# Middle and backward of an attention block in a fixed order: side work in small parts, quarter products, prefetch into dead tiles

## The chip, the cores and the metric

The kernel runs on one core of one Trainium2 chip; the chip's other cores are idle. The metric is the device time of one execution in microseconds (us). A number of executions is made, and the median is given with its range. The span of a profile is one execution, from its first to its last instruction.

Engines: PE is the matmul engine (PEld its weight loads), DVE the vector engine, ACT the scalar engine, POOL the engine that starts the output stores here, SP the engine that starts most loads. A profile lists each engine's instructions in order of time, with the idle time before each and what ended it.

## The reference, cut to what matters

One token goes through a modulated block with attention over a cache of 8192 positions, 32 heads of 192 numbers, all in bf16. The kernel returns the output and nine gradients.

```python
mod = silu(c) @ w_mod                       # w_mod: 640 x 3840, six vectors of 640
sa, ca, ga, sb, cb, gb = split(mod, 6)
h  = layernorm(x) * (1 + ca) + sa
q  = h @ wq                                 # wq: 640 x 6144
p  = softmax(q . K / sqrt(192))             # K, V: 32 x 8192 x 192
x  = x + ga * ((p @ V) @ wo)                # wo: 6144 x 640
h  = layernorm(x) * (1 + cb) + sb
x  = x + gb * mlp(h)                        # mlp holds w3: 640 x 1536, w4: 1536 x 640
# (that is the forward; then the gradients)
out, vjp = jax.vjp(f, x, K, V, wq, wo, w3, w4, c, w_mod)
return out, *vjp(grad_out)
```

Most bytes are K and V (100.7 MB each), read in the forward. The backward reads V again and writes dK and dV, of the same sizes. In all 347.74 MB are read from HBM and 226.43 MB written.

## The kernel before: the parts that matter

A cache of one head is handled in two halves, 128 partitions x 32 positions x 192 (1.5 MB). There are 64 half heads. The kernel has three stages: the forward over all heads; the "middle", which does the MLP and its backward on single vectors; and the backward over the half heads.

The names in the extracts: `V_` is DVE, `A_` ACT, `T_` PE. `P` = 128, `D` = 640, `DH` = 192, `JH` = 32, `HQ` = 32, `NT` = 16 pairs of heads, `ND` = 5, `NF` = 12, `CW` = 768 columns of a weight tile, `PW` = 384.

The middle loads w3 and w4 and reduces d(g) on DVE, twelve times:

```python
with tc.tile_pool(name="mid", bufs=1) as mid, tc.tile_pool(name="mst", bufs=2) as mst:
    w3_sb = mid.tile([P, ND, F], BF16, name="w3_sb")
    nc.sync.dma_start(out=w3_sb, in_=B_w3.rearrange("(i p) n -> p i n", p=P))
    ...                                            # w4_sb likewise; w3 transposed on PE
    bcast_cols(dbo, ND, dbo_bc, A_.copy)
    for a in range(NF):
        junk = mst.tile([P, D], BF16, name="junk")
        V_.tensor_tensor_reduce(out=junk, in0=w4_sb[:, a, :], in1=dbo_bc, scale=1.0, scalar=0.0,
                                op0=ALU.mult, op1=ALU.add, accum_out=d_g[:, a : a + 1])
    ...                                            # layer norms, MLP, their backward, dw3, dw4
```

One half head of the backward. The scheduler of the language decides the order of instructions on each engine, the program order gives only the dependencies and a preference:

```python
for h in range(HQ):
    for t in range(2):
        v = load_v(h, t)                           # 1.5 MB
        dP = tcol(JH, "dP")
        dot_sum(dot_tree(dot_mul(v, doh), psR, DH), dP)   # DVE product, PE adds 12 slices, DVE reduces
        V_.scalar_tensor_tensor(out=dS4, ...)      # (dP - cpr) * E
        dV = ob.tile([P, JH, DH], BF16, name="dV", tag="o")
        outer_v(dV, load_er(h, t), doh)            # 32 matmuls on PE, 8 copies on ACT
        nc.gpsimd.dma_start(out=dV_hd[h][:, js, :], in_=dV)
        dK = ob.tile([P, JH, DH], BF16, name="dK", tag="o")
        times(dK, qh, dS4, 0, JH)                  # DVE
        nc.gpsimd.dma_start(out=dK_hd[h][:, js, :], in_=dK)
        for f in side.get(2 * h + t, ()):          # side work of this half head
            f()
```

The side work is: `do` (dO of the next two heads: wo tile, 15 transposes, matmuls), `dq` (a tile of wq: transposes, matmuls, an outer product, dwq), `dwo`, and `wm` (a tile of w_mod, treated as one of wq). The tile of wq or w_mod has only one buffer:

```python
def load_w(view3, lo, hi):
    w = wst.tile([P, ND, CW], BF16, name="w_st", tag="w", bufs=1)      # 0.98 MB
    nc.sync.dma_start(out=w[:, :, 0 : hi - lo], in_=view3[:, :, lo:hi])
    return w

def half_chunk(view, n, b, v3, rows, dst, acc, lay):
    lo = n * CW
    if b == 0:
        cur["w"] = load_w(view, lo, lo + CW)
        cur["stg"] = bst.tile([P, ND, CW], BF16, name="stg")
    ...
    outer_chunk(cur["w"][:, :, sl], v3, rows, cur["stg"][:, :, sl], acc, lay)   # transposes w on PE, ...
    if b == 1:
        nc.gpsimd.dma_start(out=dst[:, :, lo : lo + CW], in_=cur["stg"])
```

Of the kernel before, what the change touches and what calls it, by code (L numbers as in the profile page):

```python
# [20 lines left out]
def kernel(  # L21
# [47 lines left out]
    assert DH == 192 and HQ % 4 == 0 and J % 16 == 0 and JH * TS <= 512  # L69
    assert D % P == 0 and F % P == 0 and NMOD % CW == 0  # L70
# [7 lines left out]
    pp = ctx.enter_context(tc.tile_pool(name="pp", bufs=1))  # L78
    PS = bass.MemoryType.PSUM
    psB = ctx.enter_context(tc.tile_pool(name="psB", bufs=1, space=PS))  # L80
    psS = ctx.enter_context(tc.tile_pool(name="psS", bufs=1, space=PS))
    dram = ctx.enter_context(tc.tile_pool(name="dram", bufs=1, space=bass.MemoryType.DRAM))
# [32 lines left out]
    def mean_cols(src, groups, name):  # L115
        n = groups * ND
        ps = psS.tile([P, 16], FP32, name="mean_ps", tag="s")
        T_.matmul(ps[:, 0:n], lhsT=onesD, rhs=src, start=True, stop=True)
        m = tcol(groups, name)
        V_.reduce_sum(out=m, in_=ps[:, 0:n].rearrange("p (a b) -> p a b", b=ND), axis=AX.X)  # L120
        return m

    def layernorm(x, name):
        m = mean_cols(x, 1, name + "_m")
# [4 lines left out]
        var = mean_cols(sq, 1, name + "_v")  # L129
# [125 lines left out]
    dbo = col(ND, "dbo")  # L255

# [25 lines left out]
    NKB = 5  # L282
    NVA = (7 * JQ) // 16
    MO = 256
    with tc.tile_pool(name="kp", bufs=1) as kp, tc.tile_pool(name="vs", bufs=3) as vsp, tc.tile_pool(name="ft", bufs=2) as ft, \
            tc.tile_pool(name="psM", bufs=2, space=PS) as psM, tc.tile_pool(name="psO", bufs=2, space=PS) as psO, \
            tc.tile_pool(name="psR", bufs=2, space=PS) as psR:
        KB = [None] * NKB
        for k in range(NKB):
            b = (2 * (HQ - 1) + 2 + k) % NKB  # L290
            KB[b] = kp.tile([P, JH, DH], BF16, name=f"KB{b}")

# [94 lines left out]
        ORDER = {mybir.EngineType.PE, mybir.EngineType.DVE, mybir.EngineType.Activation, mybir.EngineType.SP}  # L387
# [7 lines left out]
        with tc.manual_schedule(engines=ORDER):  # L395
            for i in range(HQ + 2):
                x = X.get(i)
# [34 lines left out]
                if x is not None:  # L432
                    x["v"].append(load_v(i, 1))
                if z is not None:
                    mt = m_out(i - 2, z["mp"], z["op"], os_)
# [33 lines left out]
                if i % 4 == 0 and mb < NMB:  # L469
                    nb = min(CW // P, NMB - mb)  # L470
                    wch = load_w(wm_v, mb * P, (mb + nb) * P)
                if y is not None:
                    m_quarter(2, y["k"][1], vs, y["mp"], y["op"])
                if x is not None:
                    dot_sum(x["d0"], x["S"][:, 0:JH])
                if y is not None:
                    y["vs"] = scale_v(3, y["v"][1], E4, Ef)
                if nx is not None:
                    nx["v"].append(load_v(i + 1, 0))
            while mb < NMB:  # L480
                nb = min(CW // P, NMB - mb)
                mod_blocks(mb, nb, load_w(wm_v, mb * P, (mb + nb) * P))
                mb += nb
    V_.tensor_tensor(out=dbo, in0=dy_c, in1=gb, op=ALU.mult)
# [8 lines left out]
    ckS = col(NQ, "ckS")  # L493
    psV = ctx.enter_context(tc.tile_pool(name="psV", bufs=2, space=PS))
    psR = ctx.enter_context(tc.tile_pool(name="psR2", bufs=1, space=PS))
    psT = ctx.enter_context(tc.tile_pool(name="psT", bufs=1, space=PS))
    with tc.tile_pool(name="mid", bufs=1) as mid, tc.tile_pool(name="mst", bufs=2) as mst:
        w3_sb = mid.tile([P, ND, F], BF16, name="w3_sb")
        nc.sync.dma_start(out=w3_sb, in_=B_w3.rearrange("(i p) n -> p i n", p=P))
        w4_sb = mid.tile([P, NF, D], BF16, name="w4_sb")  # L500
        nc.sync.dma_start(out=w4_sb, in_=B_w4.rearrange("(a p) r -> p a r", p=P))
        w3T = mid.tile([P, NF, D], BF16, name="w3T")
        for g in range(0, NF, 3):
            tp = psV.tile([P, 2048], BF16, name="w3T_ps", tag="v")
            for a in range(3):
                for k in range(ND):
                    T_.transpose(out=tp[:, a * D + k * P : a * D + (k + 1) * P], in_=w3_sb[:, k, (g + a) * P : (g + a + 1) * P], identity=ident_bf)
            A_.copy(out=w3T[:, g : g + 3, :], in_=tp[:, 0 : 3 * D].rearrange("p (a r) -> p a r", a=3))
        dbo_bc = mid.tile([P, D], BF16, name="dbo_bc")
        bcast_cols(dbo, ND, dbo_bc, A_.copy)  # L510
        d_g = mid.tile([P, NF], FP32, name="d_g")
        for a in range(NF):
            junk = mst.tile([P, D], BF16, name="junk")
            V_.tensor_tensor_reduce(out=junk, in0=w4_sb[:, a, :], in1=dbo_bc, scale=1.0, scalar=0.0, op0=ALU.mult, op1=ALU.add, accum_out=d_g[:, a : a + 1])

        ao = mid.tile([P, ND], FP32, name="ao")
        V_.reduce_sum(out=ao, in_=AO, axis=AX.X)
        x1 = mid.tile([P, ND], FP32, name="x1")
        V_.tensor_tensor(out=x1, in0=ga, in1=ao, op=ALU.mult)
        V_.tensor_tensor(out=x1, in0=x1, in1=x_c, op=ALU.add)  # L520
        n1, r1 = layernorm(x1, "ln1")
        h_b = mid.tile([P, ND], FP32, name="h_b")
        V_.scalar_tensor_tensor(out=h_b, in0=cb, scalar=1.0, in1=n1, op0=ALU.add, op1=ALU.mult)
        V_.tensor_tensor(out=h_b, in0=h_b, in1=sb, op=ALU.add)
        n2, r2 = layernorm(h_b, "ln2")
        n2_bf = tcol(ND, "n2_bf", BF16)
        V_.tensor_copy(out=n2_bf, in_=n2)
        ups = psS.tile([P, NF], FP32, name="u_ps", tag="s")
        for a in range(NF):
            for k in range(ND):  # L530
                T_.matmul(ups[:, a : a + 1], lhsT=w3_sb[:, k, a * P : (a + 1) * P], rhs=n2_bf[:, k : k + 1], start=(k == 0), stop=(k == ND - 1))

        def fcol(name, dtype=FP32):
            return mid.tile([P, NF], dtype, name=name)

        u, u2, w_, s_, g_, du = (fcol(n) for n in ("u", "u2", "w_", "s_", "g_", "du"))
        V_.tensor_copy(out=u, in_=ups)
        V_.tensor_tensor(out=u2, in0=u, in1=u, op=ALU.mult)
        V_.tensor_scalar(out=w_, in0=u2, scalar1=GELU_K1, scalar2=1.0, op0=ALU.mult, op1=ALU.add)
        V_.tensor_tensor(out=w_, in0=w_, in1=u, op=ALU.mult)  # L540
        A_.activation(out=w_, in_=w_, func=ACT.Exp, scale=-2.0 * GELU_K0)
        V_.tensor_scalar(out=w_, in0=w_, scalar1=1.0, scalar2=None, op0=ALU.add)
        V_.reciprocal(out=s_, in_=w_)
        V_.tensor_tensor(out=g_, in0=s_, in1=u, op=ALU.mult)
        g_bf = fcol("g_bf", BF16)
        A_.copy(out=g_bf, in_=g_)

        t_, v_ = fcol("t_"), fcol("v_")
        V_.tensor_scalar(out=t_, in0=s_, scalar1=-2.0 * GELU_K0, scalar2=2.0 * GELU_K0, op0=ALU.mult, op1=ALU.add)
        V_.tensor_tensor(out=t_, in0=t_, in1=g_, op=ALU.mult)  # L550
        V_.tensor_scalar(out=v_, in0=u2, scalar1=3.0 * GELU_K1, scalar2=1.0, op0=ALU.mult, op1=ALU.add)
# [285 lines left out]
```

## Time and profile before

The time is 1517.53 us (median of three runs, 1516.53 to 1517.59). The profiled execution has a span of 1520.6 us.

| stage | DMA share | GB/s | PE clock granted |
|---|---|---|---|
| forward, 80 to 540 us | 1.00 | 404 | 0.99 |
| middle, 560 to 660 us | 0.58 | 208 | 0.68 |
| backward, 700 to 1440 us | 0.98 | 393 | 0.57 |

The table is taken from the view of stage windows of the kernel before. Its columns are: the window, its length, the busy time (and instructions) of PE, PEld, DVE, ACT and POOL, then the granted clock of PE, the share of the 16 DMA engines, and GB/s.

```profile
80.00:540.00 460.00, 424.49 (x6207) 326.99 (x6206) 433.88 (x403) 337.55 (x1071) 7.72 (x14) 0.99 1.00 404
560.00:660.00 100.00, 62.62 (x776) 43.92 (x777) 49.27 (x141) 44.21 (x95) 9.94 (x16) 0.68 0.58 208
700.00:1440.00 740.00, 578.92 (x3509) 200.24 (x3509) 478.36 (x575) 404.50 (x550) 75.87 (x132) 0.57 0.98 393
```

The forward keeps the DMA engines full (1.00). The middle leaves them partly idle (0.58), so time cut from it should be time won. The backward has the DMA engines at 0.98, with PE busy 78% at a granted clock of 0.57.

The chain of waits of the kernel before, from 540 to 760 us (start, length, what held up the end at that time), shows what the middle waits for:

```profile
576.97 11.57 DMA w_sb<-in_B_w_dram
...
595.13 0.73 DVE junk L514
...
596.61 0.74 DVE junk L514
```

After the forward's last matmuls the load of w3 and w4 stands alone on the chain for 11.57 us, and the twelve d(g) reductions follow at 0.74 us each, about 9 us.

The groups of waits of the kernel before, from 655 to 1505 us (engine, line, what it waited for: us in total, times, longest us):

```profile
DVE dP L279 <- PE dot_ps L275: 242.0, 60, 16.9
...
PE wT_ps L628 <- DMA w_st<-in_w_mod_dram: 26.8, 4, 16.2
...
PE wT_ps L628 <- DMA w_st<-in_A_wq_dram: 13.5, 3, 8.4
```

DVE waits 242 us for the sums on PE. In four places PE waits for a tile of w_mod and in three for one of wq, 40.3 us in all. The timeline of the kernel before shows the longest of them (start, length, engine, line, operation, in brackets the idle time before it and what ended it):

```profile
741.57 0.38 SPq L182 DMA_DIRECT2D w_st<-in_w_mod_dram  x1
...
766.23 1.04 PE L628 MATMUL wT_ps<-ident_bf,w_st 128*128 128x128 bf16 x8 [16.20 <-DMA w_st<-in_w_mod_dram]
```

A load of 0.98 MB that is issued at 741.57 feeds its first matmul at 766.23, 24.7 us later.

A half head of the backward ends with its store of dK, so the starts of the 64 dK stores, read from the timeline of POOL, give 63 periods. Before, the first store is at 655.2 us and the last at 1504.8: a mean period of 13.49 us.

### The profile page before, as it was taken

Reading aid. Unit: us, or ns where it says so; the run is one execution under the profiler, and the core shown is the slowest. Engines: PE = TensorE matmul, PEld = TensorE weight load, DVE = VectorE, ACT = ScalarE, POOL = GpSimd, SP = SyncE. Lnnn points to the kernel's source line nnn. Section 1 sums busy time; section 2 is a strip of 40 time slices with the busy share of each in tenths; the row PEclk is TensorE's granted clock in tenths of the full one; section 3 lists DMA queues with packets and bytes.
Section 4 is the critical chain, followed back from the end, with each engine's and each line's share of the span. In section 5 each row is a group of like instructions: output and inputs, shape, how many; then the busy total and the mean of one; then the engine's idle time right before and its main releaser. Section 6 shows DMA issues by size and latency. Waiting matters only on the chain.

```text
span 1520.6 us, 28209 instructions
## 1 busy us (share of the span) xinstructions
PE 1209.5 (80%) x11811; PEld 645.4 (42%) x11811; DVE 1105.0 (73%) x1273; ACT 895.9 (59%) x1948; POOL 108.0 (7%) x193
## 2 busy tenths in 40 slices
PE   3999999998999995477668788776887788777773
PEld 1776777776776775233223223222222222222210
DVE  5999999999999975476747576675656666667663
ACT  1776777767776774255445556554555555545554
POOL 0000000000000000101001010110100010110011
PEclk7999999999999997566655555675555555556555
DMA  9999999999999985498989999999999999999978
GB/s 379 401 402 419 414 414 406 398 398 402 391 414 399 390 331 208 161 366 338 427 351 368 404 395 410 418 423 387 381 385 378 404 364 379 375 402 404 401 309 357
DMA packets 76478, 575.99 MB, mean 379 GB/s; under 512 B 7327, under 2 KB 25071, under 8 KB 35391
## 3 DMA queue, kind: packets, MB, share of 16 engines
q1 hardware_dynamic: 51530, 347.23, 57.6%
q0 software_dynamic: 24288, 226.44, 36.4%
q8 instruction: 92, 1.51, 0.4%
q10 hardware_dynamic: 532, 0.53, 0.1%
q14 instruction: 36, 0.29, 0.0%
HBM read 347.74 MB, written 226.43 MB: 378 GB/s over the span
## 4 chain that ended last, share of the span: by engine, by line
issue 33%; PE 23%; DVE 22%; ACT 10%; DMA 7%; POOL 4%; SPq 0%; POOLq 0%; ACTq 0%; DVEq 0%
DVE prod L264 11%; PE dot_ps L275 10%; ACT vs L319 5%; DVE prod L269 3%; DVE vs L312 3%; PE mp L326 3%; DMA w_st<-in_w_mod_dram 2%; PE dv_ps L737 2%; DVE S_h L279 2%; ACT dV L738 2%; PE mp L330 2%; PE wT_ps L628 2%; POOL out_dram L799 1%; POOL out_dram L796 1%; DMA w_st<-in_A_wq_dram 1%
## 5 line engine op out<-in xcount | busy, mean ns | idle before, releaser
L275 PE MATMUL dot_ps<-prod,ident_bf 128*128 128x512 bf16 x1152 | 464.9, 532 | 86.6 <-DVE prod L269 46.5
L738 ACT CAST dV<-dv_ps 128x768 bf16<-128x768 f32 x512 | 387.9, 809 | 211.0 <-PE dv_ps L737 198.5
L319 ACT ACTIVATE vs<-v_sb,Ef 128x192 bf16<-128x192 bf16 x896 | 323.4, 443 | 0.0
L737 PE MATMUL dv_ps<-do_bc,er_b 1*128 1x192 bf16 x2048 | 221.3, 327 | 57.4 <-ACT dV L738 56.7
L275 PEld LDWEIGHTS <-ident_bf 128*128 128x128 bf16 x1152 | 115.7, 114 | 265.5 <-issue 232.1
L279 DVE TENSOR_REDUCE dP<-dot_ps 128x32 f32<-128x512 f32 x64 | 44.2, 690 | 245.4 <-PE dot_ps L275 245.3
L264 DVE TENSOR_TENSOR prod<-KB,qs_bc 128x6144 bf16<-128x6144 bf16 x64 | 214.4, 3350 | 9.9 <-DMA KB<-in_A_k_cache_dram 5.5
L742 DVE TENSOR_TENSOR dK<-qs_bc,dS 128x6144 bf16<-128x6144 bf16 x64 | 214.1, 3346 | 8.2 <-DMA out_dram<-dK 8.1
L264 DVE TENSOR_TENSOR prod<-v_sb,do_bc 128x6144 bf16<-128x6144 bf16 x64 | 214.2, 3347 | 3.5 <-ACT do_bc L679 3.5
L326 PE MATMUL mp<-vs,KB 128*128 128x193 bf16 x2048 | 198.8, 250 | 0.5 <-ACT vs L319 0.5
L737 PEld LDWEIGHTS <-er_b 1*128 1x128 bf16 x2048 | 64.9, 102 | 295.7 <-issue 293.0
L326 PEld LDWEIGHTS <-KB 128*128 128x128 bf16 x2048 | 178.6, 99 | 20.6 <-issue 6.0
L312 DVE TENSOR_TENSOR vs<-v_sb,E 128x1728 bf16<-128x1728 bf16 x128 | 131.7, 1050 | 0.7 <-ACT E L300 0.6
L269 DVE TENSOR_TENSOR prod<-prod 128x3072 bf16<-128x3072 bf16 x64 | 112.1, 1751 | 0.6
L330 PE MATMUL mp<-vs,KB 128*64 128x193 bf16 x2048 | 109.8, 250 | 0.0
L628 PE MATMUL wT_ps<-ident_bf,w_st 128*128 128x128 bf16 (+1 forms) x470 | 51.8, 289 | 70.9 <-DMA w_st<-in_w_mod_dram 26.8
L330 PEld LDWEIGHTS <-KB 128*64 128x64 bf16 x2048 | 82.0, 109 | 20.8 <-issue 20.8
L796 POOL DMA_DIRECT2D out_dram<-dV x64 | 35.4, 554 | 669.9 <-ACT dV L738 669.9
L629 ACT COPY wqT<-wT_ps 128x1024 bf16<-128x1024 bf16 (+1 forms) x52 | 50.4, 970 | 49.0 <-PE wT_ps L628 39.6
L628 PEld LDWEIGHTS <-w_st 128*128 128x128 bf16 (+1 forms) x470 | 37.7, 132 | 91.3 <-issue 47.4
L300 ACT ACTIVATE E<-S_h,negm 128x256 bf16<-128x256 f32 x32 | 16.3, 508 | 91.1 <-DVE negm L421 91.1
L334 PE MATMUL op<-vs,ones_bf 128*32 128x193 bf16 x2048 | 66.2, 250 | 0.0
(207 smaller groups left out, 863.1 us busy)
## 6 DMA issues: line engine op xcount, KB each, us to landing
v_sb<-in_A_v_cache_dram SPq DMA_DIRECT2D x128, 1536.0 KB
KB<-in_A_k_cache_dram SPq DMA_DIRECT2D x64, 1536.0 KB
out_dram<-dV POOLq DMA_DIRECT2D x64, 1536.0 KB, 9.2
out_dram<-dK POOLq DMA_DIRECT2D x64, 1536.0 KB, 13.3
w_st<-in_A_wq_dram SPq DMA_DIRECT2D x16, 960.0 KB
wo_st<-in_A_wo_dram SPq DMA_DIRECT2D x32, 480.0 KB
out_dram<-stg POOLq DMA_DIRECT2D x13, 960.0 KB, 14.5
w_st<-in_w_mod_dram SPq DMA_DIRECT2D x8, 960.0 KB
```

The lines of the kernel that those rows point to most:

```text
L264: V_.tensor_tensor(out=prod, in0=src, in1=vec[:, None, :].to_broadcast([P, JH, DH]), op=ALU.mult)
L269: V_.tensor_tensor(out=prod[:, :, 0:w], in0=prod[:, :, 0:w], in1=prod[:, :, w : 2 * w], op=ALU.add)
L275: T_.matmul(ps, lhsT=ident_bf, rhs=prod[:, :, k : k + TS], start=(k == 0), stop=(k == w - TS))
L279: V_.reduce_sum(out=dst, in_=ps, axis=AX.X)
L312: V_.tensor_tensor(out=vs[:, 0:n, 0:DH].rearrange("p j (a b) -> p j a b", b=4), in0=v[:, v0 : v0 + n, :].rearrange("p j (a b) -> p j a b", ...
L319: A_.activation(out=vs[:, k, 0:DH], in_=v[:, v0 + k, :], func=ACT.Copy, scale=Ef[:, j0 + k : j0 + k + 1])
L326: T_.matmul(mp[:, 0:MW], lhsT=kb[:, j0 + k, 0:P], rhs=vs[:, k, 0:MW], start=(q == 0 and k == 0), stop=(z and k == JQ - 1), skip_group_chec ...
L330: T_.matmul(mp[p0 : p0 + 64, MO : MO + MW], lhsT=kb[:, j0 + k, P:DH], rhs=vs[:, k, 0:MW], start=False, stop=(z and k >= JQ - 2), skip_grou ...
L628: T_.transpose(out=tp[lo:hi, (x - x0) * P : (x - x0 + 1) * P], in_=src, identity=ident_bf)
L737: T_.matmul(ps[:, b, k * DH : (k + 1) * DH], lhsT=er[p0 : p0 + 1, 2 * m + k, :], rhs=doh[p0 : p0 + 1, :], start=True, stop=True)
L738: A_.copy(out=dV4[:, 2 * q : 2 * q + 2, m * PW : (m + 1) * PW], in_=ps[:, :, 0:PW])
L742: V_.tensor_tensor(out=out3[:, n0_:n1_, :].rearrange("p j (a b) -> p j a b", b=4), in0=vec.rearrange("p (a b) -> p a b", b=4)[:, None, :, ...
```

## The change: intent and diff

The change tries four things. (1) In the middle, d(g) moves into the last head of the forward, and w3, w4, the first wo tiles and three V tiles are loaded early, into K tiles that have died. (2) The backward's product is made in two quarters, so that the next half head's sum on PE may run beside this half head's dK on DVE. (3) The side work is cut into small parts, and these are dealt evenly over four slots in each half head. (4) The order of the instructions on PE, DVE, ACT and SP is fixed to the order of the program (`manual_schedule`) for the middle and the backward, too.

The core of the diff (`...` marks cuts):

```diff
+    KB = [kp.tile([P, JH, DH], BF16, name=f"KB{b}") for b in range(NKB)]
+    KX, KY, KC, KD, KE = (KB[(2 * HQ + k) % NKB] for k in (-4, -5, -3, -2, -1))
+    OB = (KE, KC, KY, KX)                        # the output tiles of the backward
+    do_bc = flat(KD)[:, 0:QD]
     ...
+            def dg_part(n):
+                for a in dgs[:n]:
+                    V_.tensor_tensor_reduce(out=junk, in0=w4r(a), in1=dbo_bc, ..., accum_out=d_g[:, a : a + 1])
+                del dgs[:n]
             for i in range(HQ + 2):
+                if i == HQ:
+                    ...                          # loads of w4, w3, a V tile, wo; d_bo broadcast
     ...
+                if i == HQ:
+                    dg_part(6)
                 if y is not None:
                     m_quarter(2, y["k"][1], vs, y["mp"], y["op"])
     ...
                 if y is not None:
                     y["vs"] = scale_v(3, y["v"][1], E4, Ef)
+                if i == HQ:
+                    dg_part(6)
     ...
+    ctx.enter_context(tc.manual_schedule(engines=ORDER))
     ...
+    def next_w():
+        if wseq:
+            view, n = wseq.pop(0)
+            cur["next"] = load_w(view, n * CW, (n + 1) * CW)
     ...
+    def g_chunk(b, v3, rows, dst, n, acc, lay):  # five parts, one per yield
+        if b == 0:
+            cur["w"] = cur.pop("next")
+        ...
+        yield
+        transposed(0, cols, ND, wT)              # part 2: first read of the weight tile on PE
+        ...
+        yield
+        transposed(8, cols, ND, wT)              # part 3: last read
+        if b == 1:
+            next_w()                             # the next tile's load, into the same buffer
+        ...
+        yield
+        ...                                      # parts 4 and 5
     ...
+    for t in range(NT):
+        if t > 0:
+            jobs.append((1, g_dwo(t)))
+        if t + 3 < NT:
+            jobs.append((3, g_do(t + 3)))
+        jobs.append((5, g_dq(t)))
+        if t % 2 == 0:
+            wseq.append((wq_v, t // 2))
+        if t % 4 == 3 and late:
+            wseq.append((wm_v, late[0]))
+            jobs.append((10, g_wm(late.pop(0))))
     ...
+    SLOTS = 4 * (NS - 5)
+    def slot():                                  # deals the side parts out evenly
+        prog[0] += 1
+        while prog[1] * SLOTS < NP * prog[0] and prog[1] < NP:
+            next(side)
+            prog[1] += 1
     ...
+    for s in range(NS):
+        ...                                      # reduction of dP, dS
+        slot()
+        dv_groups(dV, er, doh, (0, 1, 2, 3))
+        if nxt:
+            mul_q(s + 1, 0)                      # quarter product of the next half head, on DVE
+            tree_q(ps, 0)                        # its sum, on PE
+        slot()
+        dk_part(dK, qh, dS4, 0, JQ)
+        dv_groups(dV, er, doh, (4, 5))
+        slot()
+        dv_groups(dV, er, doh, (6, 7))
+        nc.gpsimd.dma_start(out=dV_hd[h][:, ...], in_=dV)
+        if nxt:
+            mul_q(s + 1, 1)
+            tree_q(ps, 1)
+        if s + 4 < NS:
+            v_l[s + 4] = load_v((s + 4) // 2, s % 2)
+        if s + 2 < NS:
+            er_l[s + 2] = load_er(s + 2)
+        dk_part(dK, qh, dS4, JQ, JH)
+        nc.gpsimd.dma_start(out=dK_hd[h][:, ...], in_=dK)
+        slot()
```

## The prediction

> **What bounds the kernel now.** The slices and stage windows show three stages.
> - Forward, 80-540 us: DMA share 1.00, 404 GB/s, TensorE clock 0.99. DMA-bound; the change does not touch it.
> - Middle, 560-660 us: DMA share 0.58, 208 GB/s. The chain of waits holds the load of w3/w4 (11.6 us after the last forward matmul), twelve d(g) reductions of 0.74 us on DVE (595.1-604.1), then dw3/dw4/dO preparation. The first dV goes out at 650.7 us, the first dK at 655.2.
> - Backward, 700-1440 us: DMA share 0.98, 393 GB/s; clock 0.57 (many slices 0.50[...]). Stores of dK run from 655.2 to 1504.8, 63 periods of 13.5 us. With no side work (1434-1483) a period is still 12.3 us at DMA share about 0.83: a serial chain of product (3.35), PE tree interleaved with dV matmuls (about 7.8), reduction 0.69, dS 0.34. DVE waits 234 us there for the tree. Side work adds stalls to that chain, and one 18.7 us hole (674-692) in which a w_mod load and side matmuls block PE.
>
> Best 10-80 us windows of the backward give 420-427 GB/s, so 393 is not the ceiling ([...]the trace comes to 427).
>
> **What the change does, costed.**
> 1. Middle: d(g) goes to the last head, where DVE is a third busy: -9 us. w3/w4, three V tiles and wo are prefetched into dead K tiles: about -3 us. dw3, du broadcast, dwo, x2 leave the path; dw4 goes to ACT (12 x about 0.5 us, off the chain). Against it: dn waits behind transposes, h2 matmuls sit before the layer-norm backward on PE (about +2). I put the first dV store at 622 us and the first dK at 626: -28 us.
> 2. Backward: quarter products (two of 1.7 us) let the next half's tree run beside this half's dK. Engine work per half stays: PE about 11 us cold (tree 5.1, dV 3.4, side 2.5), ACT 8.5, DVE 9.3. In the new order I estimate a PE-to-ACT-to-PE chain of about 12.2 us with side parts.
> 3. DMA then binds. About 342 MB remain for 64 halves, 5.34 MB each: 12.6 us at 424 GB/s, 13.2 at 405. I take 13.0: -31 us over 63 periods.
> 4. End: the last dK's landing, 15.8 us before, about 14: no large change. er loads join the SP queue: no cost expected while V prefetch runs ahead.
>
> Sum: 626 + 63 x 13.0 + 14 = 1459, with a little less if the first halves run in the DMA's slack: **1455 us** (-4%). Range 1428-1488.
>
> Chances: faster by over 2%: 0.88; within 2%: 0.10; slower: 0.02.
>
> **What the profile would show.** First dV store near 622 (wrong if after 635). d(g) off the middle's chain. Backward windows at DMA share 1.0 and 405-425 GB/s, clock still 0.5-0.6, period 12.8-13.2 us; DVE's wait for the tree falls from 234 us below 120; waits for output-tile stores appear on ACT and DVE; no hole like 674-692. Forward unchanged within 3 us.
>
> **What would make it wrong.** A saturated rate that is 390 rather than 415 with stores at 60% of the traffic (then about 1485). The fixed order making PE wait for an ACT copy of a side part, with the clock at 0.50 throughout: an engine-bound period over 13.3. SP's ordered queue holding a V load behind a weight or er load. On the other side: a warmer clock and 425 GB/s, about 1430.

"Cold" and "a warmer clock" mean no more here than a lower and a higher granted clock in the traces: 0.50 from 1434 to 1483 us, where the view gives a DMA share of 0.80 rather than 0.83, and 0.57 from 700 to 1440 us. The 5.1 us of the tree and the 3.4 us of dV fit PE's pace in the first of these stretches: from 1447.04 us on, four dV matmuls pass in 0.43 us and then five of the tree in 2.25 us, so 32 and 12 of them take 3.4 and 5.4 us by my estimate. The 0.5 us for a dw4 instruction on ACT was an estimate; the trace of the changed kernel has them at 0.82 us.

## The result, and the profile after

The changed kernel takes 1497.40 us (median of four runs, 1496.22 to 1498.64), and the kernel before, in the same rounds, 1517.56 (1516.53 to 1520.06). The ratio is 0.9865, with a 95% interval of 0.9848 to 0.9882. Ratios in this text are the mean time of one kernel's fast runs over that of the other's of the same rounds, so they are not quite the ratio of the medians that are quoted. The gain is 1.35%, where 4% was predicted, and 1497 lies outside the range.

The stage windows of the changed kernel, with two slices of 20 us beneath:

```profile
80.00:540.00 460.00, 424.34 (x6182) 326.55 (x6181) 436.49 (x405) 338.92 (x1076) 7.69 (x14) 0.99 1.00 405
560.00:660.00 100.00, 72.15 (x847) 53.19 (x845) 55.27 (x123) 58.69 (x123) 7.79 (x13) 0.70 0.68 253
700.00:1440.00 740.00, 518.41 (x4244) 310.58 (x4242) 499.75 (x736) 399.63 (x559) 80.60 (x138) 0.59 0.97 393
...
1000.00:1020.00 20.00, 7.46 (x55) 4.36 (x54) 6.99 (x9) 6.91 (x10) 1.09 (x2) 0.50 0.94 392
1020.00:1040.00 20.00, 15.91 (x129) 9.82 (x128) 12.42 (x16) 11.85 (x17) 1.05 (x2) 0.59 0.73 267
```

The forward is unchanged, the middle is denser, and the backward moves the same 393 GB/s as before. In the slice from 1000 to 1020 us PE, DVE and ACT are busy 35 to 37% of the time, and in the next one the DMA engines go down to 0.73 of their time and 267 GB/s.

The stores of dK split the span into the start (up to the first store), the 63 periods, and the drain (from the last store to the end):

| kernel | first dK store | 63 periods, sum | mean | median | over 20 us | drain | span |
|---|---|---|---|---|---|---|---|
| before | 655.2 | 849.6 | 13.49 | 12.9 | six, 20.2 to 28.5 | 15.8 | 1520.6 |
| predicted | 626 | 819 | 13.0 | | | 14 | 1459 |
| after | 630.1 | 854.8 | 13.57 | 12.9 | 23.1, 23.6, 27.8 | 10.2 | 1495.2 |

From before to after, the start is 25.0 us shorter, the backward 5.2 us longer, the drain 5.6 us shorter: 25.4 us of span. Against the prediction the start is 4 us longer, the backward 36 us longer, and the drain 4 us shorter. The three long periods exceed the median by 10.2 + 10.7 + 14.9 = 35.8 us. So the miss has the size of three holes.

The groups of waits of the changed kernel, from 655 to 1505 us, name what they are:

```profile
DVE vrow L774 <- PE bc_t L772: 98.2, 22, 15.0
DVE dP L290 <- PE dot_ps L695: 86.5, 53, 5.1
...
DVE KB L711 <- DMA out_dram<-KB: 37.3, 11, 6.0
...
PE wT_ps L582 <- DMA w_st<-in_w_mod_dram: 33.5, 3, 14.9
...
PE wT_ps L582 <- DMA w_st<-in_A_wq_dram: 2.2, 1, 2.2
```

DVE's wait for the sums on PE fell from 242.0 to 86.5 us, as the quarter products intended. But in three places PE waits for a w_mod tile, up to 14.9 us. These three waits add to 33.5 us, close to the 35.8 us by which the long periods exceed the median. All waits of PE for weight tiles were 40.3 us before and are 35.7 now: the change hardly touched them. A wait of DVE for the small transpose (bc_t) that PE issues right after the tile's transposes grew as well, from 17.9 us before to 98.2. The timeline of the changed kernel around the first of the three:

```profile
992.69 0.38 SPq L188 DMA_DIRECT2D w_st<-in_w_mod_dram  x1
...
1003.08 0.56 POOL L938 DMA_DIRECT2D out_dram<-KB  x1 [4.91 <-ACT KB L707]
...
1013.75 1.03 PE L582 MATMUL wT_ps<-ident_bf,w_st 128*128 128x128 bf16 x8 [9.18 <-DMA w_st<-in_w_mod_dram]
...
1014.88 1.01 ACT L583 COPY wT<-wT_ps 128x1024 bf16<-128x1024 bf16 x1 [12.09 <-PE wT_ps L582]
1015.03 0.28 DVE L774 CAST vrow<-bc_t 3x128 bf16<-3x128 f32 x1 [12.97 <-PE bc_t L772]
...
1026.47 0.53 POOL L938 DMA_DIRECT2D out_dram<-KB  x1 [22.05 <-ACT KB L707]
```

One late tile stops four engines in a row. PE has the transposes next in its stream and waits 9.18 us. ACT has the copy of their result next and waits 12.09; DVE has the copy of bc_t next and waits 12.97; POOL has no output to store for 22.05 us. The period is 23.1 us, 10.2 over the median, which is about PE's wait. Work that did not depend on the tile stood behind these instructions: the sums for DVE's next dP were done on PE by 1004.57 us (1001.83 + 2.74 in the same timeline), yet its reduction began at 1015.24, behind the copy of bc_t; PE's next dV matmuls began at 1016.79, behind the transposes, and ACT's next dV copies at 1018.05, behind the copies of the transposes. The three tiles take 21.1, 21.1 and 24.9 us from issue to first use.

The end of the forward, in the timelines of first the kernel before and then the changed one:

```profile
563.61 0.51 ACT L300 ACTIVATE E<-S_h,negm 128x256 bf16<-128x256 f32 x1 [0.49 <-DVE negm L421]
...
581.01 0.32 DVE L517 TENSOR_REDUCE ao<-AO 128x5 f32<-128x160 f32 x1 [0.90 <-ACT AO L456]
```

```profile
565.32 0.51 ACT L314 ACTIVATE E<-S_h,negm 128x256 bf16<-128x256 f32 x1 [0.90 <-DVE negm L459]
...
578.40 1.05 DVE L326 TENSOR_TENSOR vs<-v_sb,E 128x1728 bf16<-128x1728 bf16 x1
...
579.51 1.99 PE L340 MATMUL mp<-vs,KB 128*128 128x193 bf16 x16 [3.14 <-DVE vs L326]
...
587.39 0.32 DVE L605 TENSOR_REDUCE ao<-AO 128x5 f32<-128x160 f32 x1 [0.90 <-ACT AO L496]
```

From the last softmax to the reduction of the attention's output it was 17.4 us and is 22.1. The chain of waits of the changed kernel (start, length, what) says why:

```profile
575.05 0.83 DVE w4b L414
...
577.65 0.82 DVE w4b L414
578.49 0.98 DVE vs L326
```

These are d(g) reductions, now in the last head. They stand on the chain ahead of the last scaling of V, for which PE then waits 3.14 us.

### The profile page after: what moved, and what is told of

The parts are those of the page before. It is cut to its first block, busy times and chain, and to the rows that moved or that the text cites. A ratio compares the mean times of both kernels' runs of the same rounds, so it can differ in the third digit from the quotient of the medians.

```text
span 1495.2 us, 30163 instructions
## 1 busy us (share of the span) xinstructions
PE 1143.8 (77%) x12579; PEld 773.2 (52%) x12579; DVE 1121.6 (75%) x1391; ACT 891.5 (60%) x1966; POOL 106.7 (7%) x190
## 4 chain that ended last, share of the span: by engine, by line
issue 52%; DVE 19%; PE 12%; ACT 9%; POOL 6%; DMA 1%; POOLq 0%; SPq 0%; DVEq 0%; ACTq 0%
DVE prod L275 9%; ACT vs L333 6%; DVE vs L326 4%; DVE prod L280 3%; PE mp L340 3%; PE dot_ps L286 2%; POOL out_dram L938 2%; POOL out_dram L948 2%; DVE S_h L290 2%; PE mp L344 2%; PE q_ps L248 1%; PE op L348 1%; DMA KB<-in_A_k_cache_dram 1%; PE po L378 1%; POOL out_dram L796 1%
## 5 line engine op out<-in xcount | busy, mean ns | idle before, releaser
L707 ACT CAST KB<-dv_ps 128x768 bf16<-128x768 f32 x512 | 377.3, 813 | 167.5 <-PE dv_ps L706 152.9
L695 PE MATMUL dot_ps<-pq,ident_bf 128*128 128x256 bf16 x1536 | 327.9, 398 | 57.9 <-DVE pq L686 57.9
L706 PE MATMUL dv_ps<-KB,er_b 1*128 1x192 bf16 x2048 | 179.2, 319 | 145.2 <-ACT KB L707 137.0
L695 PEld LDWEIGHTS <-ident_bf 128*128 128x128 bf16 x1536 | 203.4, 136 | 161.3 <-issue 90.0
L711 DVE TENSOR_TENSOR KB<-qs_bc,dS 128x3072 bf16<-128x3072 bf16 x128 | 223.8, 1749 | 37.4 <-DMA out_dram<-KB 37.3
L686 DVE TENSOR_TENSOR pq<-v_sb,KB 128x3072 bf16<-128x3072 bf16 x128 | 223.7, 1748 | 0.0
L275 DVE TENSOR_TENSOR prod<-KB,qs_bc 128x6144 bf16<-128x6144 bf16 x64 | 214.5, 3352 | 10.2 <-DMA KB<-in_A_k_cache_dram 5.5
L583 ACT COPY wT<-wT_ps 128x1024 bf16<-128x1024 bf16 x84 | 81.0, 964 | 200.6 <-PE wT_ps L582 197.2
L286 PE MATMUL dot_ps<-prod,ident_bf 128*128 128x512 bf16 x384 | 97.3, 391 | 46.6 <-DVE prod L280 46.6
L344 PEld LDWEIGHTS <-KB 128*64 128x64 bf16 x2048 | 82.8, 110 | 21.1 <-issue 21.1
L582 PE MATMUL wT_ps<-ident_bf,w_st 128*128 128x128 bf16 (+1 forms) x470 | 51.7, 293 | 44.0 <-DMA w_st<-in_w_mod_dram 33.5
L286 PEld LDWEIGHTS <-ident_bf 128*128 128x128 bf16 x384 | 36.0, 99 | 89.4 <-issue 60.5
L774 DVE CAST vrow<-bc_t 3x128 bf16<-3x128 f32 x26 | 7.2, 278 | 98.2 <-PE bc_t L772 98.2
L938 POOL DMA_DIRECT2D out_dram<-KB x64 | 36.4, 569 | 589.5 <-ACT KB L707 589.3
## 6 DMA issues: line engine op xcount, KB each, us to landing
out_dram<-KB POOLq DMA_DIRECT2D x128, 1536.0 KB, 13.1
```

The costliest lines, as they stand in the source:

```text
L275: V_.tensor_tensor(out=prod, in0=src, in1=vec[:, None, :].to_broadcast([P, JH, DH]), op=ALU.mult)
L286: T_.matmul(ps, lhsT=ident_bf, rhs=prod[:, :, k : k + TS], start=(k == 0), stop=(k == w - TS))
L344: T_.matmul(mp[p0 : p0 + 64, MO : MO + MW], lhsT=kb[:, j0 + k, P:DH], rhs=vs[:, k, 0:MW], start=False, stop=(z and k >= JQ - 2), skip_grou ...
L686: V_.tensor_tensor(out=pq[:, q], in0=v_l[s][:, q * JQ : (q + 1) * JQ, :], in1=do_bc[:, None, (s // 2) * DH : (s // 2 + 1) * DH].to_broadca ...
L695: T_.matmul(ps[:, q * JQ : (q + 1) * JQ, :], lhsT=ident_bf, rhs=pq[:, q, :, k : k + TS], start=(k == 0), stop=(k == DH - TS), skip_group_c ...
L706: T_.matmul(ps[:, b, k * DH : (k + 1) * DH], lhsT=er[p0 : p0 + 1, 2 * m + k, :], rhs=doh[p0 : p0 + 1, :], start=True, stop=True)
```

## The experiments

Twelve kernels were run. Unless it is said otherwise, each differs from the changed kernel in one thing and gives the reference's result. "Over 20 us" counts the long periods between dK stores in the profiled execution.

| run | median us (range) | ratio to before [95%] | mean period | median period | over 20 us |
|---|---|---|---|---|---|
| the change again | 1498.43 (1491.18-1500.69) | 0.9857 [0.9829, 0.9885] | 13.62 | 12.8 | 3 |
| e1_fill | 1498.74 (1496.47-1504.58) | 0.9903 [0.9869, 0.9938] | 13.56 | 13.3 | 3, elsewhere |
| e2_act_ring | 1518.79 (1513.45-1527.37) | 1.0029 [0.9989, 1.007] | 14.04 | 12.8 | 7 |
| e3_split_rings | 1497.19 (1492.20-1500.00) | 0.9878 [0.9849, 0.9906] | 13.57 | 13.0 | 3 |
| e4_dg_order | 1490.98 (1489.62-1499.40) | 0.9852 [0.9818, 0.9886] | 13.63 | 12.9 | 3 |
| e5_spread | 1474.42 (1470.78-1478.37) | 0.9725 [0.9691, 0.9759] | 13.21 | 13.0 | 1 |
| e6_no_quarters | 1494.34 (1491.23-1496.88) | 0.9855 [0.9826, 0.9884] | 13.49 | 13.1 | 4 |
| e7_one_slot | 1504.40 (1498.69-1507.90) | 0.9930 [0.9896, 0.9963] | 13.53 | 13.4 | 1 |
| e8_free_order | 1491.86 (1488.76-1493.09) | 0.9836 [0.9809, 0.9864] | 13.45 | 12.1 | 6 |
| e9_one_w_load | 1456.63 (1454.89-1463.91) | 0.9599 [0.9572, 0.9626] | 12.89 | 12.9 | 1 |
| e10_half_rows | 1507.56 (1506.61-1508.51) | 0.9943 [0.9911, 0.9975] | 13.75 | 12.8 | 3 |
| c1_all | 1464.39 (1459.46-1469.80) | 0.9646 [0.9621, 0.9672] | 13.08 | 13.0 | 1 |

**Theory A:** the three holes cost the miss. In the fixed order a tile of w_mod is asked for in part 3 of the job before it and read first in part 2 of its own. Where the two jobs are neighbours, parts 4, 5 and 1 lie in between. By a count of the job list there are 206 side parts for 236 slots, and four slots in 12.9 us, so a part comes every 3.7 us by my estimate (12.9 / 4 x 236 / 206). Counting from part 3, four parts are about 15 us, and the three late tiles needed 21 to 25. A wq tile has a `dwo` and a `do` job in between as well, four parts more, about 30 us. That fits with the waits: three w_mod tiles show them, and of the wq tiles one, for 2.2 us. The trace has the distances too. PE came to the three late tiles 11.9, 11.7 and 10.0 us after their issue (first use less the wait); the wq tiles were first read 18.3 to 30.1 us after. A fourth w_mod tile with a neighbour, issued at 812.76 us, was first read after 15.6 us without a wait, for its load was quicker (see e2, e3 and e10). **Rival B:** the holes are covered, because the DMA is full anyway and catches up; the backward is bound by some 393 GB/s. **Rival C:** it is the quarter products, the slots or the fixed order that cost more on the engines than they give.

### The changed kernel again

This was run beside later experiments, to have a fresh comparison in the same rounds.

> The changed kernel itself once more, as the control for the runs beside it: 1495 to 1500 and three periods over 20 us at the three w_mod loads, if the holes belong to the order and not to one execution.

It came out at 0.9857, against 0.9865 at first, with three holes again (23.2, 25.6 and 26.9 us). The result repeats.

### e1_fill: filler jobs between neighbouring weight tiles

```diff
+    def fill(n_do, n_dwo): ...                   # appends that many do jobs, then dwo jobs
+    for n in range(NT // 2):
+        fill(*((2, 0), (1, 1), (2, 0), (1, 1), (2, 0), (1, 1), (1, 1), (0, 3))[n])
+        wseq.append((wq_v, n))
+        jobs.append((5, g_dq(2 * n)))
+        jobs.append((5, g_dq(2 * n + 1)))
+        if n % 2 == 1 and late:
+            fill(1, 1)
+            wseq.append((wm_v, late[0]))
+            jobs.append((10, g_wm(late.pop(0))))
```

> Same work as the changed kernel, only the order of the side jobs differs: the dwo and dO jobs are placed as fillers between the last read of one weight tile and the first use of the next, so each weight load has about 6 parts (some 22 us) instead of 2 to 4 to land. Theory A (the fixed order stops every engine when a weight load lands late; three periods of 23.1, 23.6 and 27.8 us against a median of 12.9 cost about 36 us): no period over 19 us, PE's wait for the w_mod load under 5 us, time 1461 to 1472. Rival B (the DMA is the ceiling and the holes only hide in it): the other periods stretch, time stays at 1487 or above.

The time did not fall: 1498.74 us. Taken alone, this would speak for rival B. The trace says otherwise. The holes at the w_mod tiles were gone, and the 47th dK store came at 1240.8 us instead of 1263.5, 22.7 us ahead. Then three new holes came. The timeline of this run:

```profile
1245.58 0.57 POOL L818 DMA_DIRECT2D out_dram<-stg_o  x1 [3.38 <-DVE stg_o L817]
...
1259.21 0.98 DVE L817 TENSOR_SCALAR stg_o<-dao_bc,o_col 128x640 bf16<-128x640 bf16 x3 [12.26 <-DMA out_dram<-stg_o]
```

I had put `dwo` jobs next to each other, and they share one staging tile. The next one has to wait until the store of the one before has landed, 12.26 us here, and DVE stands still. The wait view of this run counts 40.6 us for it. So the experiment swapped one hole for another; it had a confounder of my own making, which e5 takes away.

### e5_spread: the fillers without neighbouring `dwo` jobs

`o` stands for a `do` job of three parts, `w` for a `dwo` job of one part, `-` for an empty part.

```diff
+    for n in range(NT // 2):
+        fill(("", "ow", "ow", "owo", "ow", "owo", "ow", "owo")[n])
+        wseq.append((wq_v, n))
+        jobs.append((5, g_dq(2 * n)))
+        fill("w" if n in (1, 3, 5) else "")
+        jobs.append((5, g_dq(2 * n + 1)))
+        if n % 2 == 1 and late:
+            fill("ow")
+            wseq.append((wm_v, late[0]))
+            jobs.append((10, g_wm(late.pop(0))))
+    fill("w")
     ...
+    for n in range(GX):
+        fill("-" if n == 0 else "--w--")
         wseq.append((wm_v, n))
         jobs.append((10, g_wm(n)))
```

> Mends the confound of the filler run, where the weight-load holes vanished but three jobs in a row that share one staging tile made three new holes (each waited 12 us for a store to land). Here every gap before a weight tile's first use still holds 4 or more parts, but no two jobs of the staging tile follow each other. Theory A (any wait in the fixed order that outlasts the gap stops all engines, and the holes cost their excess over a normal period): no period over 19 us, time 1458 to 1472. Rival B (the DMA ceiling hides the holes): time 1487 or above with no hole left.

The same work, in another order of side jobs, takes 1474.42 us: 0.9725 of before, where the change has 0.9857 to 0.9865. In the wait view no w_mod tile is waited for. The stage window of this run, and its one wait for a weight tile:

```profile
700.00:1440.00 740.00, 533.41 (x4360) 321.31 (x4361) 512.59 (x737) 411.51 (x576) 82.33 (x142) 0.61 0.99 406
```

```profile
PE wT_ps L582 <- DMA w_st<-in_A_wq_dram: 6.5, 1, 6.5
```

The backward goes from 393 to 406 GB/s. Theory A is shown in its main part: taking away the three waits gave 23 us by the medians (1497.40 less 1474.42), or 1.3 to 1.4% of before by the ratios, about 20 us. The time is still 2 us above the range that was expected. Rival B falls for this order: the lost DMA time in the holes was not caught up. How the waits went is less clear-cut. The three tiles were now first read 24.0, 26.3 and 27.7 us after issue, and their loads also landed sooner, in 9.0, 10.6 and 6.0 us, with fewer store rows beside them (35, 61 and 14; see e2, e3 and e10). So e5 shows what the waits cost, and not that distance alone cures them. (In c1 the second of the three landed after 22.7 us and was read after 31.5, without a wait.) One period of 24.5 us is left, at the first wq tile, whose distance I had emptied myself; and a wait for the store of dw3 falls in the same period.

### e2_act_ring, e3_split_rings, e10_half_rows: why does the tile need 21 us?

A load of 0.98 MB that takes over 20 us moves less than 50 GB/s. I asked whether it stood behind the V loads in SP's queue (e2: the tile is started from ACT's queue; e3: three of its five row blocks from ACT, two from SP), or whether it gets turns by rows among the other transfers (e10: two loads of half the columns, so twice as many rows of half the length; the same bytes).

```diff
 # e2
-            cur["next"] = load_w(view, n * CW, (n + 1) * CW)
+            nc.scalar.dma_start(out=w, in_=view[:, :, n * CW : (n + 1) * CW])
 # e3
+            nc.scalar.dma_start(out=w[:, 0:3], in_=view[:, 0:3, n * CW : (n + 1) * CW])
+            nc.sync.dma_start(out=w[:, 3:ND], in_=view[:, 3:ND, n * CW : (n + 1) * CW])
 # e10
+            for lo in (PW, 0):
+                nc.sync.dma_start(out=w[:, :, lo : lo + PW], in_=view[:, :, n * CW + lo : n * CW + lo + PW])
```

> The changed kernel with only the weight loads of the backward issued from the ACT queue instead of SP. Theory A1 (the load is slow, 21 us for 960 KB, because it moves as 640 rows of 1.5 KB which take turns with 12 KB rows of stores): landing stays near 20 us, holes stay, time within 1% of the changed kernel. Rival A2 (it is late because it stands behind a 1.5 MB V load in SP's queue): landing falls by 5 us or more, the periods over 20 us vanish, time 1482 or less.

> The changed kernel with each weight load of the backward split by rows: three fifths on the ACT queue, two fifths on SP. Theory A1 (turn by turn with the store rows): half as many turns, so landing near 12 us, PE's waits for w_mod fall from 33 us to under 12 us, time 1470 to 1485. If instead the bytes or the queue position set the landing time: it stays near 20 us and the time within 0.5% of 1497.

> The changed kernel with each weight tile of the backward loaded by two transfers of half the columns on the same SP queue (the half that is read second goes first): the same bytes in the same place, but 1280 rows of 768 bytes instead of 640 of 1536. Theory A1 (a ring's rows take turns with the 12 KB rows of the stores, so a load's landing time follows its number of rows; the split over two rings left it at 20 us because a V load stood in front on one of them): landing of the first-read half near 40 us instead of 21, holes at nearly every weight tile, 1560 or more. If bytes or the depth of the queue set the landing time: 21 us, 1495 to 1505.

The timelines of e2, e3 and e10, in this order, at the first of the three tiles:

```profile
1003.49 0.37 ACTq L731 DMA_DIRECT2D w_st<-in_w_mod_dram  x1
...
1029.81 1.03 PE L582 MATMUL wT_ps<-ident_bf,w_st 128*128 128x128 bf16 x8 [15.93 <-DMA w_st<-in_w_mod_dram]
```

```profile
999.41 0.38 SPq L732 DMA_DIRECT2D w_st<-in_w_mod_dram  x1
...
999.50 0.41 ACTq L731 DMA_DIRECT2D w_st<-in_w_mod_dram  x1
...
1019.42 1.03 PE L582 MATMUL wT_ps<-ident_bf,w_st 128*128 128x128 bf16 x8 [9.69 <-DMA w_st<-in_w_mod_dram]
```

```profile
990.13 1.34 SPq L732 DMA_DIRECT2D w_st<-in_w_mod_dram  x2
...
1014.94 1.03 PE L582 MATMUL wT_ps<-ident_bf,w_st 128*128 128x128 bf16 x8 [13.06 <-DMA w_st<-in_w_mod_dram]
```

From issue to use it is 26.3 us on ACT's queue, 20.0 on both, 24.8 with twice the rows, and 21.1 in the changed kernel. A place behind the V loads in SP's queue is thus not the reason. Started from ACT's queue, the load still shared the time with the stores: from 1009 to 1014 us of e2, 162 of its packets stand against 162 of theirs. e2 is 1.4% slower than the change, which neither of its two theories had: it has seven long periods, and at the tile above PE waited 15.93 us. (e10 was timed in one round only; that is two runs.)

At first sight e10 speaks against the turns by rows as well: twice the rows should have brought about 40 us and brought 24.8. The DMA records of the same traces say otherwise. This is the view of the DMA queues, of the changed kernel from 997 to 1003 us and of e10 from 1006 to 1012 us (queue, kind: packets, MB, share of the 16 engines); q0 holds POOL's stores, q1 SP's loads, and nearly all packets of q1 in these stretches are rows of the weight tile:

```profile
q0 software_dynamic: 197, 2.22, 87.4%
q1 hardware_dynamic: 196, 0.30, 13.3%
```

```profile
q0 software_dynamic: 205, 2.33, 91.2%
q1 hardware_dynamic: 203, 0.22, 10.2%
```

Packet for packet, loads and stores take turns in these stretches (196 against 197), and a row of half the length gets no more turns (203 against 205). In e2 it is the 162 against 162 above; in e3, with the load on two queues (1004 to 1010 us), 178 against 177 and 176. At 196 packets in 6 us, 640 rows take about 20 us by my estimate. e10 did not take 40 because the stores ran out: while its 1280 rows passed, only 468 store rows of 12 KB and some 300 smaller packets did, and where no stores ran its rows went faster (in the changed kernel, the tile issued at 1036.51 us had no store row beside it and landed after 4.7 us). e3's load, expected to land near 12 us, landed after 18.9: its first row came 4.0 us after issue, and ACT's three fifths are 384 rows. So the turns by rows stand, and the landing time follows the stores that run at the same time. Of the 13 weight tiles in the changed kernel's backward, seven had 0 to 78 such store rows beside them and landed 4.7 to 10.8 us after issue; six had 193 to 424 and landed after 18.2 to 24.0 us. The three late tiles are among the six.

### e9_one_w_load: is it the DMA's ceiling?

This is e5 with all later weight tiles reusing the first one: 12 loads, 11.8 MB, fewer. Its result is wrong (the gradient of c alone, which sums over the real w_mod), and its instructions are the same ones.

```diff
-            cur["next"] = load_w(view, n * CW, (n + 1) * CW)
+            if "one" not in cur:
+                cur["one"] = load_w(view, n * CW, (n + 1) * CW)
+            cur["next"] = cur["one"]
```

> The spread-filler kernel with only the first weight tile of the backward loaded; the other twelve loads (0.98 MB each, 11.8 MB) are left out and the chunks read that one tile, so its weight gradients' partner sums are wrong on purpose. If without holes the DMA is the ceiling (0.99 share, 406 GB/s): the time falls by what these bytes take, 11.8 MB / 406 GB/s = 29 us, to 1440 to 1452. If the engines' chain sets the 13.2 us period: 1465 or more.

The time fell from 1474.42 to 1456.63, ratios 0.9725 and 0.9599. Moving 11.8 MB at 406 GB/s takes 29 us, so a purely DMA-bound backward should have won 29, and 18 came (19 by the ratios). The stage window of this run:

```profile
700.00:1440.00 740.00, 536.89 (x4484) 324.76 (x4485) 530.04 (x750) 424.19 (x594) 84.33 (x146) 0.63 0.98 398
```

The DMA share is 0.98 now and the rate 398 GB/s, less than in e5: with fewer bytes to move the DMA no longer sets the pace alone, and the mean period of 12.89 us (13.21 in e5) seems to come from the engines' chain as well. (The time lies between the two ranges that were expected.) I take it that the DMA's limit and the chain of the engines lie within some 3% of each other once the holes are gone; this is inferred, as no run made the engines' part shorter without the holes.

### e6_no_quarters, e7_one_slot, e8_free_order: the other parts of the change

e6 makes both quarter products and both sums together at the end of the half head. e7 calls all four slots at the end. e8 drops the line that fixes the order, and leaves all else.

```diff
 # e6
-            mul_q(s + 1, 0)                      # (was between the dV groups)
-            tree_q(ps, 0)
-            mul_q(s + 1, 1)
-            tree_q(ps, 1)
+            for q in range(2):
+                mul_q(s + 1, q)
+            for q in range(2):
+                tree_q(ps, q)
 # e7
-        slot()                                   # (four calls, spread)
+        for _ in range(4):
+            slot()
 # e8
-    ctx.enter_context(tc.manual_schedule(engines=ORDER))
```

> The changed kernel with the products of the next half made at the end of the half (both quarters, then both trees) instead of one in the middle and one at the end. If the chain product, tree, reduction still bounds the backward, as the prediction had it for the old kernel, the median period rises from 12.9 to 13.5 or more and the time to 1525 or more. If the period is set by the DMA and by the holes (theory A), the time stays within 0.7% of 1497.

> The changed kernel with the same number of side parts per half, but all of them at the end of the half instead of in four slots. If small parts in four slots keep PE and ACT from waiting on each other: median period up by 0.5 us or more, time 1515 or more. If the DMA sets the period and the slots are only cosmetic: within 0.7% of 1497.

> The changed kernel with the middle and the backward handed back to the scheduler: same instructions, same tiles, no fixed order after the forward. If the fixed order is what turns a late weight load into a stop of every engine (theory A): the three periods over 23 us shrink below 20, time 1470 to 1490. If the fixed order is a gain in itself, as the change intends: the middle grows and the time is 1505 or more.

e6 comes out at 0.9855, the same as the change. Nothing measurable is lost without the quarters, in a backward that is held by holes and by the DMA between them. Whether they are worth something once the holes are gone was not run.

e7 is slower, 0.9930. Its median period is 13.4 instead of 12.9, which is what the spread of the slots gives; but the waits at the three w_mod tiles vanish. PE came later to two of the three (11.4, 21.7 and 19.9 us after issue, against 11.9, 11.7 and 10.0 in the change). And their loads landed sooner, in 9.6, 10.2 and 8.5 us, with 70, 80 and 36 store rows beside them, where the change has 331, 382 and 424. Two effects run against each other (the sum of the periods is 852.3 us, against 854.8), so what the slots give by themselves is not settled.

e8 comes out at 0.9836, no slower than the change (0.9865 and 0.9857). The scheduler's order has six long periods, like the kernel before, and a median period of 12.1 us. Its waits for weight tiles, from 640 to 1540 us:

```profile
PE wT_ps L581 <- DMA w_st<-in_A_wq_dram: 33.6, 5, 13.0
...
PE wT_ps L581 <- DMA w_st<-in_w_mod_dram: 27.8, 3, 10.0
```

That is 61.4 us, against 35.7 in the change. So the expectation that the long periods shrink below 20 us without the fixed order failed: the fixed order is not what makes a late tile stop the engines. In the scheduler's order, too, PE waits at eight weight tiles (five of wq, three of w_mod); the same job list brings late tiles there as well. And e8 is not slower for its longer waits. At 5.34 MB per half head, 12.1 us would be 441 GB/s by my estimate, more than any window quoted here, so some bytes of the short periods must have moved in the long ones. In that order part of the lost time is caught up, as rival B had it; what a hole costs depends on the order around it. The fixed order did not win anything as such in this backward, and the first dK store is at 629.5 us without it, too. So the middle's 25 us come from the moved work and the early loads, not from the order.

### e4_dg_order: d(g) off the last head's chain

Four of the d(g) reductions go where DVE has time, and eight come after the last scaling of V.

```diff
+                if i == HQ:
+                    dg_part(4)                   # ahead of m_add
     ...
-                if i == HQ:
-                    dg_part(6)                   # was ahead of the last scaling of V
     ...
                 if i == HQ:
-                    dg_part(6)
+                    dg_part(8)
```

> The changed kernel with the twelve d(g) reductions of the last head moved: four before the M2 addition where DVE waited 4 us, eight after the last V scaling, none between the third and the fourth V scaling. Theory C (the six reductions ahead of the fourth scaling held PE for 3 us and the forward's end by 6): forward ends 4 to 6 us earlier, first dK store near 625, time 1491 to 1493 if the backward carries it through, else 1497 if the backward is bound by what happens later.

The timeline of this run, to be compared with the pair above:

```profile
567.76 0.51 ACT L314 ACTIVATE E<-S_h,negm 128x256 bf16<-128x256 f32 x1 [0.91 <-DVE negm L459]
...
585.57 0.32 DVE L605 TENSOR_REDUCE ao<-AO 128x5 f32<-128x160 f32 x1 [0.90 <-ACT AO L498]
```

The stretch is back at 17.8 us from 22.1 (before: 17.4). The first dK store moved only 1.4 us earlier, to 628.7. This run's softmax began 2.4 us later, and eight reductions are left for after; how much each of these took back was not measured. The time, 0.9852, can't be told from the change's.

### c1_all: what the findings add up to

e5, with a filler `do` job ahead of the first wq tile, dw3's parts mixed with those of `do(2)`, d(g) as four early, four late and four in the waits of the layer norms, the broadcast of d_bo behind the softmax maximum, and the small er load issued ahead of the V load.

```diff
-            def dg_part ... dg_part(6) ... dg_part(6)
+            dg_part(4) early, dg_part(4) after the last scaling of V
+    n1, r1 = layernorm(x1, "ln1", dg_w3t)        # each wait also does one d(g) reduction
-    (3, g_do(2)), (3, g_dw3())
+    (6, mix(g_dw3(), g_do(2)))
+        fill(("o", "ow", "ow", "owo", "ow", "owo", "ow", "ow")[n])
     ...
+        if s + 2 < NS:
+            er_l[s + 2] = load_er(s + 2)
         if s + 4 < NS:
             v_l[s + 4] = load_v((s + 4) // 2, s % 2)
```

(The first lines of this diff are told rather than copied; the rest is as in e5.)

> The spread-filler kernel with the rest mended too: fillers before the first weight tile, dw3 parts interleaved with a dO job, d(g) reductions in DVE's idle places of the last head and of the layer norms, the dbo broadcast after the softmax maximum and on DVE, er loads issued ahead of the V load. Theories A and C: first dK near 626, no period over 18 us, 1455 to 1466. If the first hole and the middle are absorbed by the DMA: 1470 or more.

It is correct and takes 1464.39 us: 0.9646 of before, 0.9621 to 0.9672. It beats both kernels. The stage window and the only waits for a weight tile:

```profile
700.00:1440.00 740.00, 526.20 (x4379) 318.65 (x4377) 519.25 (x741) 413.00 (x577) 82.53 (x142) 0.61 1.00 411
```

```profile
PE wT_ps L582 <- DMA w_st<-in_A_wq_dram: 9.2, 2, 7.5
```

The backward now has the DMA share at 1.00 and 411 GB/s. The first dK store is at 626.5, the mean period 13.08, the drain 10.4: 626.5 + 823.8 + 10.4 = 1460.6, the span of the profiled execution. These are almost the prediction's own terms, 626 + 819 + 14. The time lies in the expected range, but one period of 21.1 us is left where none over 18 was expected. What each of the added parts gave was not measured apart.

A second buffer for the weight tile would be the plain remedy. It does not fit: with two buffers the changed kernel does not build, because a later pool asks for 18.375 KB per partition where 15.6875 KB are left. It was not run.

## Why the prediction was wrong, and where it was right

**The step that failed** is "no hole like 674-692", together with item 3's "DMA then binds ... I take 13.0". The period of 13.0 us, 31 us off the backward, supposed that in the new order nothing waits for long. The hole that I had seen at 674 us went, but three of its kind came: PE waited 40.3 us for weight tiles before and 35.7 us after, and the mean period was 13.57 us, not 13.0. I had seen the late w_mod load in the profile before, and had read it as an accident of the scheduler's order; e8 has such waits too, and more of them (61.4 us), so who fixes the order is not the cause; e5, which only reorders the job list, takes the three waits away. The load at 741 us in the lines above needed 24.7 us to its first use beside the stores. With that figure and the diff at hand, the distance in parts could have been counted beforehand: four parts of 3.7 us are less than 21. The three holes exceed the median period by 35.8 us; the backward is 36 us longer than predicted; and with them mended (e5) 20 to 23 us come back. With the further repairs of c1 it is 33 us by the medians, some of it from the middle; the 63 periods are 31 us shorter there (823.8 us).

The listed dangers came near it and missed. "SP's ordered queue holding a V load behind a weight or er load" names the same load, with the wrong victim: PE waited for the weight itself, and e2 shows that its place in SP's queue was not the cause. "er loads join the SP queue: no cost expected" missed by little: PE waited 7.6 us for them, in two places. In c1, which issues them ahead of the V load, the view shows no such wait.

**The middle** was right in size. Predicted were the first dV store at 622 and the first dK at 626 us; they came at 633.3 and 630.1, still within the 635 named, though the dV store is 11 us late and now goes out after the dK store. But "d(g) goes to the last head, where DVE is a third busy: -9 us" was only partly right. Six of the reductions lay on the last head's chain again, and the forward's end took 22.1 us instead of 17.4. "d(g) off the middle's chain" was wrong in that sense. In e4's places the stretch is 17.8 again; in c1, which moves the d_bo broadcast too, it is 21.7 (562.26 to 583.96 us), so c1's earlier first dK store does not come from this stretch.

**The quarter products** did what was said to DVE's wait for the sums (from 242.0 to 86.5 us; predicted below 120), though its wait for bc_t grew by 80.3; and they gave no time that can be measured (e6). The step "a period is still 12.3 us ...: a serial chain" (with no side work) was a reading of the last four half heads and not of what binds the other sixty: the median period was 12.9 before and is 12.9 after. At 5.34 MB per half head, 12.9 us are 414 GB/s. That is the rate c1 holds with the DMA share at 1.00 (411). So the changed kernel seems to run at it between its holes. The kernel before has more long periods (six) and makes up part of them with short ones, so that the two means, 13.49 and 13.57, hardly differ.

**Right were** the binding by DMA once nothing else waits (c1: 1.00 and 411 GB/s, predicted 1.0 and 405 to 425), the clock (0.59 on average and 0.50 in the slice of the hole, predicted 0.5 to 0.6), the waits for output stores on DVE (37.3 us; on ACT they did not appear as forecast, 4.0 us after 9.8 before), the unchanged forward (405 against 404 GB/s). The drain was 4 us shorter than thought. As written for the changed kernel, though, "DMA share 1.0 and 405-425 GB/s" was wrong: it had 0.97 and 393.

## What to carry to other kernels

Whoever fixes the order, hand or scheduler, every load's distance to its first use has to be counted in time and compared with a landing time read under the same traffic: here the same 0.98 MB landed in 4.7 us or in 24.0, by the stores that ran beside them. With one buffer, a load can't be issued before the last read of the tile before, so other work has to lie between the neighbours. In the changed kernel one late load stopped PE for 9.18 us, and then ACT for 12.09 and DVE for 12.97 us behind it; the loss was real (23 us by the medians in e5) though the DMA is 97% busy on average, as a share over a long stretch hides holes (0.73 from 1020 to 1040 us). A filler that reuses a staging tile brings its own wait (12.26 us in e1): after each repair, look at the periods again, not just at the time.
